# The head of a fused attention and feed-forward kernel: k's squares on other engines, fp32 warm matmuls, another order of the last loads

## Chip, core and metric

One core of a Trainium2 chip runs the whole kernel. The metric is device time in microseconds. Three timed executions of the kernel before took 556.75, 556.82 and 558.07 us, median 556.82.

The engines and their names in the profile: TensorE (PE; its weight loads are PEld), VectorE (DVE), ScalarE (ACT), GpSimd (POOL) and SyncE (SP). POOL issues nearly all loads, SP the transposing DMAs and nearly all stores.

## What is computed

Four batches of 5824 rows and 256 channels. A 256 x 256 attention over channels is made from q and k, applied to v, and the result passes a feed-forward stage without a nonlinearity except one product.

```
qn = q / (norm(q, axis=1) + 1e-6)          # norms run over the 5824 rows
kn = k / (norm(k, axis=1) + 1e-6)
s  = kn^T @ qn / tau                       # 256 x 256 for each batch
a  = exp(s - max); a = a / (sum(a) + 1e-9)
x  = reshape(v @ a)                        # 23296 x 256
out = ((x @ w1) * (x @ w2)) @ w3 @ w_out
```

Inputs and output are fp32; the loads cast to bf16. tau is 1.

## The kernel before

The attention matrix is folded into the weights: for each batch `Wf` = e w1, e w2, scaled by the reciprocals of the sums, so that the main stage needs v alone; w3 and w_out are multiplied once into `W_sb`.

**Main stage.** For each batch there are 12 chunks of up to 512 rows and 8 column blocks `j`: 96 slots. A slot (`emit_ab`, L627) makes `a` and `b` = Wf-block x vT, 128 x 512 each, in two matmuls each; ScalarE casts `a` (L633), VectorE multiplies it with `b` (L644) to `abh`. The banks for `a` and `b` are four, in turn. The product of `abh` with `W_sb` follows some slots later, either plainly (L675, L706) or with seven products in place of eight (L540).

**Order.** The order on every engine is the order of the program, written by a planner: `make_agenda` files pieces of work under a planned time or, for the scores of the next batch, under a slot. The scores of batch 1 are 92 units (23 pairs of row slots, four units each; two of four hold matmuls, L200). `SLOTS0` is the first and last slot of the range over which batch 0 spreads them, and `EARLY` of them are placed before slot `EARLY_SLOT`. Loads for later batches stand in POOL's queue behind `gate` (waits for the newest `abh`) or `hold` (waits for the transpose of a piece of v).

**Head.** Batch 0 has nothing to hide its scores behind. Each of q and k comes in six pieces; pieces 0 to 4 hold 8 slots of 128 rows, piece 5 holds 5 (`LAST` = 5) and a half slot of 64 rows. A DMA waits until the DMA eight places before it in POOL's queue has landed. TensorE runs, as the pieces come:

- `squares`: t^T t of each slot in two 128 x 128 blocks, summed into `S["k"]` and `S["q"]`, whose diagonals are the squared norms (L236);
- `products`: q^T k into G (L248);
- `busy`: matmuls of zeros that only keep TensorE at work (L224).

When k is through, `k_first` multiplies `S["k"]` by the identity (L259), and `k_row` sums it over the partitions by a matmul with ones (L311) and takes four activations to 1/(norm + eps), the row `kr` (L319). `q_first` gets q's squared norms from the diagonal (L328), `q_norm` their reciprocal norms (L339 to L342), `scale` multiplies G by `kr` (L350), `exps` makes `e` (L355). `sum_mm` sums e (L375, its reciprocal L383), `quarter_mm` makes the first folds, 256 columns of w1 and of w2 at a time, which ScalarE (c1 = 0, L431) and VectorE (c1 = 1, L433) scale into `Wf`. Then slot 0 starts. The first two pieces of v are transposed by TensorE in halves (L143), evicted by VectorE (L147) or ScalarE (L145); piece 2 and later by DMA (L166).

The end of the head before, in the program:

```
squares("k", 4, whole)
for sl in (lo, hi):
    squares("q", 4, sl)
    products(4, sl)
squares("k", 5, range(LAST + 1), end=True)
soft0[0]()
parts = [[LAST, 0], [1, 2], [3], [4]]
```

**Tail.** The last half slots of batches 2 and 3 are stored from one tile by two DMAs on SP (L721), the last full row slot from ScalarE's queue (L725).

Of the kernel before, what the change touches and what calls it, by code (L numbers as in the profile page):

```python
# [9 lines left out]
AF = mybir.ActivationFunctionType  # L10
ALU = mybir.AluOpType
F32 = DT.float32
# [13 lines left out]
def kernel(  # L26
# [193 lines left out]
    def busy(k):  # L220

        m = psum.tile([P, 512], F32, name=f"warm_{nc.get_next_instruction_name()}", **bank("ab"))
        for _ in range(k):
            nc.tensor.matmul(m, lhsT=warm[:, :P], rhs=warm, start=True, stop=True, skip_group_check=True)  # L224

    S = {}

    def squares(nm, pi, slots, end=False):

        if nm not in S:  # L230
            S[nm] = psum.tile([P, CT, P], F32, name=f"sq{nm}_0", **bank("out"))
        t = pieces[nm, 0, pi]
        for i in slots:
            for ct in range(CT):
                cs = slice(ct * P, (ct + 1) * P)
                nc.tensor.matmul(  # L236
                    S[nm][:, ct, :], lhsT=t[:, i, cs], rhs=t[:, i, cs],
                    start=(pi == 0 and i == 0 and ct == 0),
                    stop=(end and i == slots[-1] and ct == CT - 1), skip_group_check=True,
                )  # L240

# [12 lines left out]
    def soft_units(n):  # L254
        st = {}

        def k_first():
            d = work.tile([P, CT, P], F32, tag="sq", name="dk", bufs=2)
            nc.vector.tensor_mul(d, S["k"], ident.unsqueeze(1).to_broadcast([P, CT, P]))  # L259
            st["ksq"] = d.rearrange("p c t -> p (c t)")  # L260

        def scaled_first():
            scale(0)
            q_norm(st["ss"])
            scale(1)
            exps(0)
            exps(1)

# [143 lines left out]
            for c2 in range(CT):  # L412
                fold_mm((w, c1, h * 512, (h + 1) * 512), c2, tag, i % 2 == 0 or (n == 0 and i == 7))

        def quarter_mm(lo, c1, c2):

            if c2 == 0:
                tag = "ab" if lo == 0 else "out"
                st[lo, c1] = psum.tile([P, 2, 256], F32, name=f"quarter_{lo}_{c1}", **bank(tag))
            m = st[lo, c1]  # L420
            for w in range(2):
                nc.tensor.matmul(
                    m[:, w, :], lhsT=st["e"][:, c2, c1 * P : (c1 + 1) * P], rhs=w12[:, c2, w, lo : lo + 256],
                    start=(c2 == 0 and w == 0), stop=(c2 == CT - 1 and w == 1), skip_group_check=True,
                )
            if c2 == CT - 1:
                for o in (0, P) if lo == 0 else (slice(0, 256),):
                    cols = slice(o, o + P) if lo == 0 else o
                    dst, src = Wf[n][:, c1, :, lo : lo + 256][:, :, cols], m[:, :, cols]
                    if c1 == 0:  # L430
                        nc.scalar.activation(out=dst, in_=src, func=AF.Copy, scale=st["rs"][:, c1 : c1 + 1])  # L431
                    else:
                        nc.vector.tensor_scalar_mul(dst, src, st["rs"][:, c1 : c1 + 1])  # L433

        def first_folds():
            sum_mm(0)
            for c1 in range(CT):
                quarter_mm(0, c1, 0)
            sum_mm(1)
            for c1 in range(CT):  # L440
                quarter_mm(0, c1, 1)

        def second_quarter():
            for c1 in range(CT):
                for c2 in range(CT):
                    quarter_mm(256, c1, c2)

        if n == 0:
            return [k_first, k_row, q_first, scaled_first, first_folds, second_quarter, sum_start] + [lambda i=i: fold(i) for i in range(4, 8)]

        return (
            [(0.0, 0.0, norms), (0.1, 2.4, totals)]
# [23 lines left out]
        agenda.append((t, seq[0], cost, fn))  # L476

    out_tiles = {}
    lefts = {}
    pend = []  # L480

# [205 lines left out]
    def emit_out(b, c, j, ab, only=None):  # L687

        small = c == NCH - 1
        if small:  # L690
            lhs = [ab[:, :P]]
            if b % 2 == 1:
                lhs.append(lefts[b // 2][:, j, :, :].rearrange("p b t -> p (b t)")[:, P : P + 2 * LEFT])
        else:
            lhs = [ab[:, i * P : (i + 1) * P] for i in range(4)]
        if j == 0:
            out_tiles[b, c] = [
                psum.tile([P, 2, D], F32, tag=tag, name=f"o_{b}_{c}_{tag}", bufs=1)
                for tag in ((("out0", "out2") if b == B - 1 else ("out0", "out1"))[: len(lhs)] if small else ("out0", "out1"))
            ]  # L700
        tl = out_tiles[b, c]
        for s, lhsT in reversed(list(enumerate(lhs))) if small and b == B - 1 else enumerate(lhs):
            if only is not None and s != only:
                continue
            h, o = (s, 0) if small else divmod(s, 2)
            nc.tensor.matmul(  # L706
                tl[h][:, o, :], lhsT=lhsT, rhs=W_sb[:, j, :],
                start=(j == 0 and o == 0), stop=(j == FT - 1 and (small or o == 1)),
                skip_group_check=True,
            )  # L710
        clock[0] += len(lhs) * (D * MM_COL + MM_FIX)
        if j == FT - 1:
            o = work.tile([P, 4, D], F32, tag="o_sb", name=f"osb_{b}_{c}", bufs=3)
            rows = out[b * N : b * N + NT * P, :].rearrange("(p i) c -> p i c", i=NT)
            if small:
                if b % 2 == 1 and only != 0:
                    o2 = work.tile([P, D], F32, tag="kr", name=f"oleft_{b}", bufs=1)
                    nc.vector.tensor_copy(o2, tl[1][:, 0, :])
                    for m in (b - 1, b):
                        k = (m - b + 1) * LEFT  # L720
                        nc.sync.dma_start(out=out[m * N + NT * P : (m + 1) * N, :], in_=o2[k : k + LEFT, :])  # L721
                if only != 1:
                    nc.scalar.copy(o[:, 0, :], tl[0][:, 0, :])
                    other = nc.scalar if b == B - 1 else nc.sync
                    other.dma_start(out=rows[:, NT - 1, :], in_=o[:, 0, :])  # L725
            else:
                nc.scalar.copy(o[:, 0:2, :], tl[0])
                nc.vector.tensor_copy(o[:, 2:4, :], tl[1])
                nc.sync.dma_start(out=rows[:, 4 * c : 4 * c + 4, :], in_=o)
            if only is None:  # L730
                del out_tiles[b, c]
# [4 lines left out]


    half = PIECE // 2
    busy(10)
    raw = {}  # L740
    for nm in "kq":
        new_piece(nm, 0, 0)
# [39 lines left out]
        load_piece("k", 0, pi)  # L782
        load_piece("q", 0, pi)
    load_piece("k", 0, 4)
    load_piece("q", 0, 4, (half,))
    load_piece("k", 0, 5)
    soft0 = soft_units(0)
    whole = range(PIECE)
    lo, hi = range(half), range(half, PIECE)
    for sl in (lo, hi):  # L790
        squares("k", 0, sl)
        busy(2)
    for sl in (lo, hi):
        squares("q", 0, sl)
        products(0, sl)
    for pi in range(1, 4):
        squares("k", pi, whole)
        if pi < 3:
            busy(2)
        squares("q", pi, whole)  # L800
        products(pi, whole)
    load_piece("q", 0, 5, (1, 3, 4))
    new_piece("v", 0, 0)
    load_part("v", 0, 0, 0, half)
# [5 lines left out]
    load_piece("v", 0, 2)  # L810
    nc.gpsimd.dma_start(out=wout_sb, in_=moe_w_out.rearrange("(lh ll) c -> ll lh c", ll=P))
    nc.gpsimd.dma_start(out=w3_bf, in_=w3r)
    squares("k", 4, whole)
    for sl in (lo, hi):
        squares("q", 4, sl)
        products(4, sl)
    squares("k", 5, range(LAST + 1), end=True)
    soft0[0]()
    parts = [[LAST, 0], [1, 2], [3], [4]]
    for i, sl in enumerate(parts):  # L820
        end = i == len(parts) - 1
        squares("q", 5, sl, end=end)
        if end:
            soft0[2]()
        products(5, sl, end=end)
        if i == 0:
            soft0[1]()
    soft0[3]()
    soft0[6]()
    busy(3)  # L830
    transpose_half_on_pe(0, 0, 0, False)
    soft0[4]()

# [9 lines left out]
        else:  # L843
            nc.vector.tensor_copy(W_sb[:, jt, :], m[:, :D])

    SLOTS0, SLOTS = (36, 78), (4, 71)
    EARLY, EARLY_SLOT = 32, 46
    COMB, W_SLOT = 39, 32
    by_slot = []

# [15 lines left out]
    def make_agenda(b):  # L866
# [3 lines left out]
        if b == 0:  # L870
            at(0.5, 0.87, soft0[5])
            for i in range(4):
                at((1.7, 2.6, 3.5, 3.9)[i], 0.43, soft0[7 + i])
            at(4.6, 0.5, lambda: transpose_half_on_pe(0, 0, 1, False))
            at(7.0, 0.5, lambda: transpose_half_on_pe(0, 1, 0, True))
            at(8.0, 0.5, lambda: transpose_half_on_pe(0, 1, 1, False))
            at(15.0, 0.0, transpose_w3)
            at(15.0, 0.0, lambda: transpose_piece(0, 2))
# [9 lines left out]
            moves = [m for m in moves if m[1] < B]  # L888

        for nm, m, pi, t in moves:  # L890
            if (nm, m, pi) in (("qk", 1, 0), ("qk", 1, 2)):
                at(t, 0.0, lambda i=2 + pi // 2: hold(vTs[0][0][:1, i * PIECE, 0, :1]))
            at(t, 0.0, gate)
            if nm == "qk":
                at(t, 0.0, lambda m=m, pi=pi: load_qk(m, pi))
            else:
                at(t, 0.0, lambda m=m, pi=pi: load_piece("v", m, pi))
                at(t + 4.0, 0.0, lambda m=m, pi=pi: transpose_piece(m, pi))
# [81 lines left out]
```

## Time and profile before

| | |
|---|---|
| profiled execution | 557.51 us |
| its span, first to last instruction | 555.5 us |
| median of three timed executions | 556.82 us |
| PE busy | 543.3 us (98% of the span) |
| DVE, ACT, POOL busy | 421.1, 366.7, 305.4 us |
| mean granted TensorE clock | 0.998 |
| first matmul of slot 0 | 37.54 us |
| first load issued by POOL | 1.23 us |

Busy is the time in which an engine had an instruction at work; it says nothing on whether that work was needed or waited for. TensorE's matmuls overlap in the records: a matmul of 128 columns lasts 219 ns, yet 16 in a row start and end within 1.06 us. So the start-to-start distance is the price of one, and the duration shows when its result is there.

A timeline line reads: start, duration, engine, line of the program, operation, written tile <- read tiles, shape, how many merged; in brackets the idle time of the engine before it, and what ended that.

The windows of the head show what each engine does there (busy us of each window):

| window, us | PE | DVE | ACT | POOL | GB/s |
|---|---|---|---|---|---|
| 0 to 10 | 7.48 | 3.27 | 2.33 | 5.66 | 212 |
| 10 to 20 | 7.80 | 0.00 | 0.00 | 2.15 | 213 |
| 20 to 30 | 8.95 | 0.00 | 0.00 | 3.39 | 208 |
| 30 to 40 | 8.64 | 4.81 | 5.13 | 6.93 | 171 |
| 40 to 50 | 9.92 | 6.89 | 7.36 | 0.00 | 208 |
| 50 to 60 | 10.00 | 7.96 | 6.66 | 0.00 | 167 |

### The profile page before, as it was taken

The page shows a single profiled execution, that of the slowest core. Times are in us where ns is not written, and L with a number is a line of the kernel's source. Part 1 is how long each engine was busy: PE and PEld are TensorE (multiplying, and loading weights), DVE is VectorE, ACT ScalarE, POOL GpSimd, SP SyncE. Part 2 cuts the span into 40 slices and gives each one's busy share as a digit, 9 for nine tenths or more (in the row PEclk, how much of TensorE's full clock was granted, in tenths as well). Part 3 has the DMA queues.
Part 4 walks back from the last instruction along what each step waited for, and adds up shares of the span by engine and source line. Part 5 has one row for each costly group of instructions (what it writes and reads, how often), then busy time and mean ns, then how long its engine had stood idle before and what let it go on. Part 6 is the DMA issues. An engine that isn't in the chain of part 4 may idle for free.

```text
span 555.5 us, 12406 instructions
## 1 busy us (share of the span) xinstructions
PE 543.3 (98%) x4697; PEld 355.7 (64%) x4697; DVE 421.1 (76%) x766; ACT 366.7 (66%) x740; POOL 305.4 (55%) x258
## 2 busy tenths in 40 slices
PE   7899999999999999999999999999999999999997
PEld 5764577666666666666667566666666666666665
DVE  2047748799976797888876688888877688888984
ACT  1046647688866877877766778787766566666663
POOL 4260020867789588898887588898977400010000
PEclk9999999999999999999999999999999999999999
DMA  9999988987566977675555767875651245343102
GB/s 212 211 182 209 159 153 199 219 181 136 127 147 153 181 148 163 134 159 131 121 127 133 153 133 167 174 142 118 153 114 39 81 110 125 87 112 84 77 39 95
DMA packets 75115, 77.60 MB, mean 140 GB/s; under 512 B 54192, under 2 KB 58800, under 8 KB 75056
## 3 DMA queue, kind: packets, MB, share of 16 engines
q0 software_dynamic: 15760, 38.93, 40.4%
q1 hardware_dynamic: 59008, 37.23, 24.0%
q8 instruction: 36, 0.59, 0.4%
q10 hardware_dynamic: 288, 0.66, 0.4%
q14 instruction: 23, 0.19, 0.1%
HBM read 78.91 MB, written 23.86 MB: 185 GB/s over the span
## 4 chain that ended last, share of the span: by engine, by line
PE 86%; DMA 9%; POOL 1%; ACT 1%; DVE 1%; issue 1%; POOLq 0%; ACTq 0%
PE a L627 27%; PE b L627 27%; PE prodA L540 12%; PE prodC L540 6%; PE G L200 5%; DMA k<-in_k_dram 4%; PE prodB L540 3%; DMA v<-in_v_dram 2%; PE fold L398 2%; DMA q<-in_q_dram 2%; PE o_out L706 2%; PE w L837 1%; DMA vT<-v 1%; POOL k L120 1%; POOL q L120 0%
## 5 line engine op out<-in xcount | busy, mean ns | idle before, releaser
L644 DVE TENSOR_TENSOR abh<-as,b 128x512 bf16<-128x512 bf16 x352 | 239.9, 684 | 85.1 <-ACT as L633 81.5
L633 ACT CAST as<-a 128x512 bf16<-128x512 f32 (+1 forms) x384 | 215.8, 563 | 93.3 <-PE a L627 63.4
L627 PE MATMUL a<-vT,Wf 128*128 128x512 bf16 x704 | 209.4, 379 | 0.4 <-ACT Wf L431 0.4
L627 PE MATMUL b<-vT,Wf 128*128 128x512 bf16 x704 | 209.4, 379 | 0.0
L627 PEld LDWEIGHTS <-Wf 128*128 128x128 bf16 x1536 | 141.4, 98 | 101.5 <-issue 0.8
L540 PEld LDWEIGHTS <-S 128*128 128x128 bf16 x1248 | 82.6, 98 | 34.3
L212 DVE TENSOR_TENSOR acc<-acc,sq 128x512 f32<-128x512 f32 x132 | 91.5, 693 | 2.7 <-ACT sq L197 1.9
L550 ACT COPY osb<-prodA 128x256 f32<-128x256 f32 x156 | 58.1, 373 | 42.7 <-PE prodA L540 42.2
L559 POOL TENSOR_TENSOR S<-abh,abh 128x1024 bf16<-128x1024 bf16 x29 | 61.8, 2131 | 31.5 <-DVE abh L644 16.4
L540 PEld LDWEIGHTS <-abh 128*128 128x128 bf16 x936 | 62.0, 98 | 25.7 <-issue 0.2
L562 POOL TENSOR_TENSOR S<-S,abh 128x1024 bf16<-128x1024 bf16 x29 | 61.7, 2128 | 1.9
L562 POOL TENSOR_TENSOR S<-abh 128x1024 bf16<-128x1024 bf16 x29 | 61.8, 2132 | 0.1
L562 POOL TENSOR_TENSOR S<-abh,S 128x1024 bf16<-128x1024 bf16 x29 | 61.8, 2133 | 0.1
L615 POOL COPY gate_t<-abh 1x1 bf16<-1x1 bf16 x39 | 7.3, 186 | 79.9 <-DVE abh L644 79.7
L200 PE MATMUL G<-k,q 128*128 128x256 bf16 x276 | 48.3, 273 | 0.9 <-DMA k<-in_k_dram 0.9
L540 PE MATMUL prodA<-comb_T,S 128*128 128x128 bf16 x624 | 47.6, 219 | 0.0
L197 ACT ACTIVATE sq<-q 128x512 f32<-128x512 bf16 x69 | 43.8, 634 | 0.0
L197 ACT ACTIVATE sq<-k 128x512 f32<-128x512 bf16 x69 | 43.5, 631 | 0.0
L553 DVE TENSOR_TENSOR osb<-prodC,osb 128x256 f32<-128x256 f32 x78 | 32.5, 417 | 0.0
L619 POOL COPY gate_t<-vT 1x1 bf16<-1x1 bf16 x2 | 0.4, 178 | 55.0 <-DVE abh L644 37.6
L200 PEld LDWEIGHTS <-q 128*128 128x128 bf16 x276 | 23.6, 98 | 4.2 <-issue 1.0
L540 PE MATMUL prodB<-W_sb,abh 128*128 128x128 bf16 x312 | 23.8, 219 | 0.1
(128 smaller groups left out, 449.6 us busy)
## 6 DMA issues: line engine op xcount, KB each, us to landing
out_dram<-osb SPq DMA_DIRECT2D x44, 512.0 KB, 3.4
k<-in_k_dram POOLq DMA_DIRECT2D x19, 512.0 KB, 8.7
v<-in_v_dram POOLq DMA_DIRECT2D x19, 512.0 KB, 5.7
q<-in_q_dram POOLq DMA_DIRECT2D x18, 512.0 KB, 5.8
w_wout<-in_moe_w_dram POOLq DMA_DIRECT2D x1, 2048.0 KB, 22.8
k<-in_k_dram POOLq DMA_DIRECT2D x4, 320.0 KB, 7.1
v<-in_v_dram POOLq DMA_DIRECT2D x4, 320.0 KB, 4.8
q<-in_q_dram POOLq DMA_DIRECT2D x3, 320.0 KB, 5.3
```

Source lines behind the costliest of these rows:

```text
L197: nc.scalar.activation(out=sqs[0][:, :, part, :], in_=src[:, o : o + 2, :], func=AF.Square)
L200: nc.tensor.matmul(G[:, ct, :], lhsT=qt[:, i, ct * P : (ct + 1) * P], rhs=kt[:, i, :], start=(pr == 0 and part == 0 and ct == 0), stop=(pr ...
L212: nc.vector.tensor_add(accs[n], accs[n], sqs[0][:, part - 2])
L398: nc.tensor.matmul(m, lhsT=st["e"][:, c2, c1 * P : (c1 + 1) * P], rhs=w12[:, c2, w, lo:hi], start=(c2 == 0), stop=(c2 == CT - 1),)
L540: nc.tensor.matmul(st[nm][:, i, :], lhsT=a[:, j, i * P : (i + 1) * P], rhs=w[j], start=(first and j == 0 and i == 0), stop=(j == 3), skip_ ...
L550: nc.scalar.copy(quarter(r, d), st["A"])
L553: nc.vector.tensor_add(quarter(r, d), st[nm], quarter(r, d))
L559: adder.tensor_add(x, a21, a22)
L562: adder.tensor_sub(x, u, w)
L627: nc.tensor.matmul(t[:, :n], lhsT=Wf[b][:, ct, w, j * P : (j + 1) * P], rhs=rhs_of(b, c, ct), start=(ct == 0), stop=(ct == CT - 1),)
L633: nc.scalar.copy(a_sb[:, :n], tiles[0][:, :n])
L644: nc.vector.tensor_mul(ab, a_sb, tiles[1])
```

## The change

1. The squares of k's slots 0 to 35 (pieces 0 to 3, and half of piece 4) leave TensorE. ScalarE squares two slots at a time, VectorE adds them into one PSUM tile `kacc`. `k_early` joins its two halves, and `k_first` adds them to the diagonal that the remaining ten slots give; the sum over partitions by `k_row` is as before.
2. The zero matmuls in bf16 are replaced by fp32 matmuls of ones with 512 columns (`busy_long`), 3 at the start, then 2, 1 and 2 behind the pieces 0, 1 and 2. The ones behind the first exponentials' inputs stay bf16, 2 instead of 3.
3. k's piece 5 is loaded ahead of the second half of q's piece 4, which comes in two parts; `k_row` stands ahead of q's piece 5.
4. Both scalings of G stand ahead of q's norm.
5. The first folds take 128 columns, evicted at once; the next 128 follow before slot 0.
6. Batch 1's scores start at slot 37 with 28 units before slot 46.
7. One TensorE transpose of v is evicted by VectorE instead of ScalarE.
8. The store of the last batch's half slot goes to ScalarE's queue behind its row store.

The two uses of `hold` stay, only written otherwise. The diff, cut:

```diff
+    def busy_long(k):
+        m = psum.tile([P, 4, P], F32, name=f"warm_{nc.get_next_instruction_name()}", **bank("ab"))
+        for _ in range(k):
+            nc.tensor.matmul(
+                m, lhsT=ones_pp, rhs=ones_pp.unsqueeze(1).to_broadcast([P, 4, P]), start=True, stop=True,
+                skip_group_check=True,
+            )
+    def add_k_squares(pi, slots):
+        for i in slots[::2]:
+            src = pieces["k", 0, pi][:, i : i + 2, :]
+            if not kacc:
+                kacc.append(psum.tile([P, 2, C], F32, name="kacc", tag="out0", bufs=1))
+                nc.scalar.activation(out=kacc[0], in_=src, func=AF.Square)
+                continue
+            sq = work.tile([P, 2, C], F32, tag="sq", name=f"ksq_{pi}_{i}", bufs=2)
+            nc.scalar.activation(out=sq, in_=src, func=AF.Square)
+            nc.vector.tensor_add(kacc[0], kacc[0], sq)
...
+        def k_early():
+            st["kk"] = work.tile([P, C], F32, tag="kk", name="kk", bufs=1)
+            nc.vector.tensor_copy(st["kk"], kacc[0][:, 0, :])
+            nc.vector.tensor_add(st["kk"], kacc[0][:, 1, :], st["kk"])
...
             nc.vector.tensor_mul(d, S["k"], ident.unsqueeze(1).to_broadcast([P, CT, P]))
-            st["ksq"] = d.rearrange("p c t -> p (c t)")
+            d = st["ksq"] = d.rearrange("p c t -> p (c t)")
+            nc.vector.tensor_add(d, d, st["kk"])
         def scaled_first():
-            scale(0)
+            for ct in range(CT):
+                scale(ct)
             q_norm(st["ss"])
-            scale(1)
...
         def first_folds():
-            sum_mm(0)
+            for c2 in range(CT):
+                sum_mm(c2)
+                for c1 in range(CT):
+                    narrow_fold(0, P, c1, c2)
             for c1 in range(CT):
-                quarter_mm(0, c1, 0)
-            sum_mm(1)
-            for c1 in range(CT):
-                quarter_mm(0, c1, 1)
+                for c2 in range(CT):
+                    narrow_fold(P, 2 * P, c1, c2)
...
-                        nc.sync.dma_start(out=out[m * N + NT * P : (m + 1) * N, :], in_=o2[k : k + LEFT, :])
+                        store = lambda m=m, k=k, queue=nc.sync: queue.dma_start(
+                            out=out[m * N + NT * P : (m + 1) * N, :], in_=o2[k : k + LEFT, :]
+                        )
+                        if m < B - 1:
+                            store()
+                        else:
+                            last_rows.append(store)
...
+                    if last_rows:
+                        last_rows.pop()(queue=nc.scalar)
...
-    busy(10)
+    busy_long(3)
...
-    load_piece("q", 0, 4, (half,))
+    new_piece("q", 0, 4)
+    load_part("q", 0, 4, 0, half)
     load_piece("k", 0, 5)
+    load_part("q", 0, 4, half, half + 2)
+    load_part("q", 0, 4, half + 2, PIECE)
...
-    for sl in (lo, hi):
-        squares("k", 0, sl)
-        busy(2)
+    add_k_squares(0, whole)
     for sl in (lo, hi):
         squares("q", 0, sl)
         products(0, sl)
+    busy_long(2)
     for pi in range(1, 4):
-        squares("k", pi, whole)
-        if pi < 3:
-            busy(2)
+        add_k_squares(pi, whole)
         squares("q", pi, whole)
         products(pi, whole)
+        if pi < 3:
+            busy_long(pi)
...
-    squares("k", 4, whole)
-    for sl in (lo, hi):
+    add_k_squares(4, lo)
+    soft0[7]()
+    squares("k", 4, hi)
+    squares("q", 4, lo)
+    products(4, lo)
+    squares("k", 5, range(LAST + 1), end=True)
+    soft0[0]()
+    for sl in (range(half, half + 2), range(half + 2, PIECE)):
         squares("q", 4, sl)
         products(4, sl)
-    squares("k", 5, range(LAST + 1), end=True)
-    soft0[0]()
-    parts = [[LAST, 0], [1, 2], [3], [4]]
...
+    soft0[1]()
+    for sl in ([LAST, 0], [1, 2], [3]):
+        squares("q", 5, sl)
+        products(5, sl)
+    squares("q", 5, [4], end=True)
+    soft0[2]()
+    products(5, [4], end=True)
     soft0[3]()
     soft0[6]()
-    busy(3)
+    busy(2)
...
-    SLOTS0, SLOTS = (36, 78), (4, 71)
-    EARLY, EARLY_SLOT = 32, 46
+    SLOTS0, SLOTS = (37, 78), (4, 71)
+    EARLY, EARLY_SLOT = 28, 46
...
-            at(7.0, 0.5, lambda: transpose_half_on_pe(0, 1, 0, True))
+            at(7.0, 0.5, lambda: transpose_half_on_pe(0, 1, 0, False))
```

More of the change, by code (lines that the diff above doesn't have):

```diff
@@ L224, in busy @@
             nc.tensor.matmul(m, lhsT=warm[:, :P], rhs=warm, start=True, stop=True, skip_group_check=True)
+    def busy_long(k):
[5 more added lines that the diff above has]
+            )
+    kacc = []
+    def add_k_squares(pi, slots):
[8 more added lines that the diff above has]
+            nc.vector.tensor_add(kacc[0], kacc[0], sq)
     S = {}
@@ L237, in squares @@
                     S[nm][:, ct, :], lhsT=t[:, i, cs], rhs=t[:, i, cs],
-                    start=(pi == 0 and i == 0 and ct == 0),
+                    start=((pi, i) == ((4, half) if nm == "k" else (0, 0)) and ct == 0),
                     stop=(end and i == slots[-1] and ct == CT - 1), skip_group_check=True,
@@ L413, in fold, with narrow_fold @@
                 fold_mm((w, c1, h * 512, (h + 1) * 512), c2, tag, i % 2 == 0 or (n == 0 and i == 7))
-        def quarter_mm(lo, c1, c2):
+        def narrow_fold(lo, hi, c1, c2):
             if c2 == 0:
-                tag = "ab" if lo == 0 else "out"
-                st[lo, c1] = psum.tile([P, 2, 256], F32, name=f"quarter_{lo}_{c1}", **bank(tag))
+                tag = "ab" if lo < 256 else "out"
+                st[lo, c1] = psum.tile([P, 2, hi - lo], F32, name=f"narrow_{lo}_{c1}", **bank(tag))
             m = st[lo, c1]
@@ L422, in quarter_mm @@
                 nc.tensor.matmul(
-                    m[:, w, :], lhsT=st["e"][:, c2, c1 * P : (c1 + 1) * P], rhs=w12[:, c2, w, lo : lo + 256],
+                    m[:, w, :], lhsT=st["e"][:, c2, c1 * P : (c1 + 1) * P], rhs=w12[:, c2, w, lo:hi],
                     start=(c2 == 0 and w == 0), stop=(c2 == CT - 1 and w == 1), skip_group_check=True,
@@ L426, in quarter_mm @@
             if c2 == CT - 1:
[L427 to L433, printed above, removed]
+                dst = Wf[n][:, c1, :, lo:hi]
+                if c1 == 0:
+                    nc.scalar.activation(out=dst, in_=m, func=AF.Copy, scale=st["rs"][:, c1 : c1 + 1])
+                else:
+                    nc.vector.tensor_scalar_mul(dst, m, st["rs"][:, c1 : c1 + 1])
         def first_folds():
-            sum_mm(0)
+            for c2 in range(CT):
+                sum_mm(c2)
+                for c1 in range(CT):
+                    narrow_fold(0, P, c1, c2)
             for c1 in range(CT):
-                quarter_mm(0, c1, 0)
-            sum_mm(1)
-            for c1 in range(CT):
-                quarter_mm(0, c1, 1)
+                for c2 in range(CT):
+                    narrow_fold(P, 2 * P, c1, c2)
         def second_quarter():
@@ L445, in second_quarter @@
                 for c2 in range(CT):
-                    quarter_mm(256, c1, c2)
+                    narrow_fold(256, 512, c1, c2)
         if n == 0:
-            return [k_first, k_row, q_first, scaled_first, first_folds, second_quarter, sum_start] + [lambda i=i: fold(i) for i in range(4, 8)]
+            return [k_first, k_row, q_first, scaled_first, first_folds, second_quarter, sum_start, k_early] + [lambda i=i: fold(i) for i in range(4, 8)]
         return (
@@ L478 @@
     out_tiles = {}
+    last_rows = []
     lefts = {}
@@ L720, in emit_out @@
                         k = (m - b + 1) * LEFT
-                        nc.sync.dma_start(out=out[m * N + NT * P : (m + 1) * N, :], in_=o2[k : k + LEFT, :])
+                        store = lambda m=m, k=k, queue=nc.sync: queue.dma_start(
[3 more added lines that the diff above has]
+                            store()
+                        else:
+                            last_rows.append(store)
                 if only != 1:
@@ L812 @@
     nc.gpsimd.dma_start(out=w3_bf, in_=w3r)
-    squares("k", 4, whole)
-    for sl in (lo, hi):
+    add_k_squares(4, lo)
[6 more added lines that the diff above has]
+    for sl in (range(half, half + 2), range(half + 2, PIECE)):
         squares("q", 4, sl)
         products(4, sl)
-    squares("k", 5, range(LAST + 1), end=True)
-    soft0[0]()
-    parts = [[LAST, 0], [1, 2], [3], [4]]
[L820 to L827, printed above, removed]
+    soft0[1]()
[5 more added lines that the diff above has]
+    products(5, [4], end=True)
     soft0[3]()
     soft0[6]()
-    busy(3)
+    busy(2)
     transpose_half_on_pe(0, 0, 0, False)
@@ L872, in make_agenda @@
             for i in range(4):
-                at((1.7, 2.6, 3.5, 3.9)[i], 0.43, soft0[7 + i])
+                at((1.7, 2.6, 3.5, 3.9)[i], 0.43, soft0[8 + i])
             at(4.6, 0.5, lambda: transpose_half_on_pe(0, 0, 1, False))
-            at(7.0, 0.5, lambda: transpose_half_on_pe(0, 1, 0, True))
+            at(7.0, 0.5, lambda: transpose_half_on_pe(0, 1, 0, False))
             at(8.0, 0.5, lambda: transpose_half_on_pe(0, 1, 1, False))
@@ L890, in make_agenda @@
         for nm, m, pi, t in moves:
-            if (nm, m, pi) in (("qk", 1, 0), ("qk", 1, 2)):
-                at(t, 0.0, lambda i=2 + pi // 2: hold(vTs[0][0][:1, i * PIECE, 0, :1]))
+            if nm == "qk" and m == 1 and pi in (0, 2):
+                at(t, 0.0, lambda pi=pi: hold(vTs[0][0][:1, (2 + pi // 2) * PIECE, 0, :1]))
             at(t, 0.0, gate)
```

## The prediction

> **What bounds the kernel now.** I read the busy table first (PE 98% of the span), then who TensorE waits for, the chain of waits of the first 75 us, and the instructions around each place where that chain leaves TensorE. After the first `a` matmul at 37.54 us TensorE loses almost nothing; the waits from there on are two (engine, what it waits for: us in total, times, longest):
>
> ```profile
> PE G L200 <- DMA k<-in_k_dram: 0.9, 1, 0.9
> PE a L627 <- ACT Wf L431: 0.4, 1, 0.4
> ```
>
> So the time is: when the first `a` starts, plus about 514 us of packed TensorE work, plus the tail. The chain of the head (start us, us, what):
>
> ```profile
> 4.51 16.54 DMA k<-in_k_dram
> 21.34 10.29 DMA q<-in_q_dram
> 31.96 0.44 PE G L248 x4
> 32.40 0.45 PE row L311 x2
> 33.73 0.52 ACT kr L319
> 35.45 0.52 ACT e L355
> ...
> 37.01 0.48 ACT Wf L431
> 37.54 0.61 PE a L627 x2
> ```
>
> Until 31.6 the loads set the pace; the DMA engines move 208 to 213 GB/s through the first 30 us, so nothing before that is worth anything unless it finishes loads earlier. From 31.6 on it is a dependent chain: last q, k's row of sums, four activations, the exponentials, first folds, first `a`. The timeline of the hand-over:
>
> ```profile
> 31.67 0.28 PE L236 MATMUL sqq<-q 128*128 128x128 bf16 x2 [0.42 <-DMA q<-in_q_dram]
> ...
> 33.66 0.28 PE L236 MATMUL sqq<-q 128*128 128x128 bf16 x2
> ...
> 33.97 0.29 DVE L328 CUSTOM_DVE_ANT_0 dq<-sqq,ident 128x128 f32<-128x128 f32 x1 [2.37 <-PE sqq L236]
> ...
> 35.45 0.91 ACT L355 ACTIVATE e<-s,r 128x256 bf16<-128x256 f32 x2 [0.44 <-DVE r L342]
> ...
> 36.57 0.60 PE L422 MATMUL quarter<-w,e 128*128 128x256 bf16 x4
> ```
>
> The last part of q was issued at 27.51 and took 5.0 us to land, so it is there at 32.5; its squares start at 33.66. For 2.0 us from 31.67 TensorE is without a gap and behind the loads.
>
> Two more places outside the head:
>
> ```profile
> 49.23 0.59 PE L627 MATMUL b<-vT,Wf 128*128 128x512 bf16 x2
> 105.33 0.60 PE L200 MATMUL G<-k,q 128*128 128x256 bf16 x4 [0.85 <-DMA k<-in_k_dram]
> 551.70 1.12 SPq L721 DMA_DIRECT2D out_dram<-oleft  x2
> 551.86 0.36 ACTq L725 DMA_DIRECT2D out_dram<-osb  x1
> ```
>
> **Part by part.**
>
> *Squares of k off TensorE.* 36 slots x 2 = 72 matmuls; 16 of them take 0.90 us (10.98 to 11.88), so 4.0 us leave TensorE. All lie before 27 us, where TensorE waits for q anyway (3.7 us in four waits): worth 0. In their place come 18 squares on ScalarE (631 ns each, the row of the later k squares, 11.4 us) and 17 adds on VectorE (693 ns, 11.8 us). Cover: VectorE sits idle 22.9 us before 31.18, ScalarE 26.2 before 32.87. The last two slot pairs hang on k piece 4, landed at 25.95 (issued 7.25, 18.7 to land): squares to 27.6, adds to 28.3, the two joining operations to about 29.1 (0.4 each, as the 128x256 multiply). k's diagonal cannot start before k piece 5, so this is hidden; were it not, each 0.7 us late would first eat the slack of the row below.
>
> *Order of loads and of the row.* Now k piece 5 comes before the second half of q piece 4. It should land near 29.0 (before: 30.28), q piece 4's two new parts at 29.7 and 30.2, the same bytes by then. TensorE: k5 squares to 29.6, first part (0.22 + 0.44) to 30.3, second to 31.0, the row (0.45) to 31.4, and q piece 5 waits for its load as before (31.64). What falls out of the gapless 2.0 us after 31.67 is the row: the final squares move from 33.66 to 33.21. POOL's queue: one more DMA, and the ninth and later issues each stand until the one eight earlier has landed. Counting on with those landings, the last weights before v go out about 0.2 us later (w3 at 36.7 instead of 36.5), since the weight issues run back to back at 0.7 us either way.
>
> *The price of the split.* The DMA records of the trace give 173 ns for a 2 KB packet, 98 for 1 KB, 60 for 512 B. Half a piece of q was 128 packets of 2 KB: 128 x 173 / 16 engines = 1.38 us; as two parts it is 256 x 98 / 16 = 1.57. By the row the q loads end 0.19 later. The Trainium skill speaks both ways: "DMA: Bandwidth & Descriptors" (Specifications) lets anything from 512 B up run at line rate, which makes it 0 and the gain 0.45; "Perfetto Trace Analysis" (DMA Optimizations) warns of overhead under 2 KB without a price, and even at the 512 B row (240 ns per 2 KB) it would be 0.5, which takes the gain away. I take the row: final squares at 33.40, 0.26 earlier.
>
> *From the last squares to e.* Now k's row is ready by 33.5, so both scalings follow the diagonal at once and the norm of q comes behind them on VectorE: diagonal from +0.31 to +0.82, scalings 0.34 apart, then add and reciprocal at the old spacing; e starts 1.93 after the squares (before 35.45 - 33.66 = 1.79). So 35.33 against 35.45: 0.12 earlier.
>
> *Narrow first folds.* The second half of the row sums waited for four 256-column matmuls (36.08 to 36.52) though e was ready at 36.36. Four of 128 columns take 0.22, so it now waits for e: 36.30 instead of 36.52. The fold in front of ScalarE's eviction shrinks too, and the reciprocal (0.21 behind the sums, 0.17 long) becomes the releaser: eviction at about 36.75 instead of 37.01. It still covers 256 elements a row (0.42). The 8 matmuls of columns 128 to 256 (0.45) fit beside it. First `a` at **37.28: 0.26 earlier**. The first weights must be there at 35.95; I put the second one's landing at 35.4.
>
> *Warm matmuls in fp32.* Eight of 512 columns; the fp32 row has 256 columns in 0.45, so 0.9 each. Except for the first three, they stand where TensorE waits for q and all end before its landing (11.4 against 13.15, 16.7 against 18.8, 23.2 against 23.5): 0. But the longest pauses grow from 1.65 us (17.16 to 18.81) to about 2.1. Before, 128 columns take 0.055 us after every pause; at the start the first warm matmuls came every 0.43 us instead of 0.216 until 4.19. The Trainium skill ("TensorE: Matmul & The Clock Gate", HAM oscillation) asks for no pause over about 3.4 us, which clears this; its next section tells of clocks that fell on short pauses, which does not. No row here has a 2.1 us pause. Between 0 and one cold stretch like the start's (2.9 us at half rate, 1.5 us lost); I take 0, near the 1.65 us row.
>
> *A transpose's eviction from ScalarE to VectorE.* Before, ScalarE's 1.01 us copy delayed its next cast, VectorE then stood 1.10 us, came late with the following product, and `b` at 49.23 started 0.20 after TensorE was free. On VectorE the copy fits that idle stretch: **-0.20**.
>
> *Scores of batch 1 paced.* 28 units instead of 32 before slot 46 move the first pair of k piece 2 from slot 46 to slot 48, about 4 us of packed work later. That load landed at 105.28 and hangs on a chain of DMAs (hold, v piece 3, its transpose, hold), which the head does not shift. TensorE gets there at 108, so the whole wait goes: **-0.85**. Next late would be k piece 3 (111.6 against slot 56, after 121): no. Starting at slot 37 protects the first pair, whose k landed at 83.4, 0.05 before use.
>
> *Tail.* The last store on SP starts at 552.24 and lands at 554.55, the row store on ScalarE's queue at 554.35. Behind the latter the moved store can start at 552.22 and ends issuing 0.24 sooner. Between -0.25 and +0.15; I take **-0.1**.
>
> **Sum**: -0.26 - 0.20 - 0.85 - 0.10 = -1.4. Against the profiled execution (557.51; span 555.5 and 2.0 around it) 556.1; that execution was 0.7 above the median, so **555.4**.
>
> **Rivals.** About 0.3% (1.67 us) is what a measurement can tell from no change.
> - *Head gain held up* (0.20): v pieces bound it. Slot 32 at 75.63 needs a transpose landed at 74.94, v piece 1 lands some 0.5 before its transpose; with loads 0.2 later little of 0.46 may pass. -0.95: 555.9.
> - *Loads end no later* (0.22): packets overlap, the split costs nothing: head -0.5 to -0.6, and stores gain their 0.25. -1.9: 554.9, faster.
> - *Clock falls at the hand-over* (0.13): between 33.7 and 37.3 TensorE has about 1.6 us of pauses (before some 1.45, with one warm matmul more), the `a` stage starts at half rate. One stretch is +1.5, a second +3.0; slower than before once over 1.4, beyond 0.3% once over 3.1. Two stretches: 558.4. For it: the thinner filling; against: nothing cold after 4.2 us before.
> - *As summed* (0.45): own range 554.9 to 556.0.
>
> Range 554.2 to 557.6. Faster by over 0.3% needs under 555.15: most of the second rival and a third of the sum's own spread, 0.33; slower 0.12; within 0.55.
>
> **What would show it.** First `a` at 37.1 to 37.4; final q squares at 33.2 to 33.4; no wait on k at L200's successor near 105; the 0.2 gap near 49 gone; 55 ns a matmul after every pause. It is wrong if q piece 5 lands after 32.2, if `a` waits for vT at slot 32, or if the first `a` and `b` run at 0.43 a matmul.

## The result, and the profile after

The changed kernel took 556.14 us (median of 15 runs, 555.53 to 556.96) against 557.38 of the kernel before beside it (15 runs, 556.58 to 558.07). The ratio is 0.9978 with a 95% interval of 0.9970 to 0.9986, or -1.24 us with an interval of -0.8 to -1.7: a small gain. The interval excludes no change, but the 0.22% lies below the 0.3% that I had put as what a measurement can tell. In the profiled executions it is 555.64 us (span 553.9) against 557.51 (span 555.5).

Who TensorE waits for in the first 38 us of the kernel after (us in total, times, longest); from 37.7 us to the end the same view names nobody, where it named k for 0.9 and ScalarE's first copy of `Wf` for 0.4 before:

```profile
PE sqq L259 <- DMA q<-in_q_dram: 4.0, 4, 1.3
...
PE sum L404 <- ACT e L384: 0.6, 1, 0.6
```

The chain of the head after (start us, us, what):

```profile
13.31 15.71 DMA k<-in_k_dram
...
30.67 5.22 DMA w<-in_moe_w_dram
...
35.93 0.33 PE narrow L451 x3
...
36.59 0.48 ACT Wf L458
...
37.12 0.61 PE a L656 x2
```

Before, the chain ran through q, k's row and `e`. Now the last thing that comes late is a weight: the second of the first weights, issued at 30.67, releases the folds at 35.89, though `e` started at 34.98. The timeline of the hand-over:

```profile
29.07 0.84 PE L259 MATMUL sqk<-k 128*128 128x128 bf16 x12 [0.24 <-DMA k<-in_k_dram]
...
33.15 0.28 PE L259 MATMUL sqq<-q 128*128 128x128 bf16 x2
...
34.98 0.91 ACT L384 ACTIVATE e<-s,r 128x256 bf16<-128x256 f32 x2 [0.54 <-DVE r L371]
...
35.61 0.65 PE L451 MATMUL narrow<-w,e 128*128 128x128 bf16 x4
```

The merged row at 35.61 hides the wait: four matmuls of 128 columns, which take 0.38 us where nothing holds them, show 0.65, and no bracket. Only the chain says why. And the three places outside the head:

```profile
48.20 0.59 PE L656 MATMUL a<-vT,Wf 128*128 128x512 bf16 x2
48.64 0.60 PE L656 MATMUL b<-vT,Wf 128*128 128x512 bf16 x2
...
107.19 0.60 PE L200 MATMUL G<-k,q 128*128 128x256 bf16 x4
550.69 0.67 ACTq L750 DMA_DIRECT2D out_dram<-oleft  x1
```

`a` and `b` near 48 are 0.43 apart, the packed distance: the gap of 0.20 is gone. The scores that waited at 105.33 now stand at 107.19, and their k landed at 103.51: no bracket. In the tail the moved store takes 0.67 us to issue.

Every span can be cut at the first `a` and at ScalarE's last copy of output. That separates the head, the packed stage and the tail, and is the measure for the experiments (us, one profile each):

| kernel | last q squares | `e` | first `a` | first `a` to last copy | last copy to end |
|---|---|---|---|---|---|
| before | 33.66 | 35.45 | 37.54 | 513.92 | 4.01 |
| before, again (e4_base) | 33.66 | 35.46 | 37.55 | 514.90 | 3.98 |
| pacing alone (e1_pace) | 33.64 | 35.47 | 37.55 | 512.93 | 4.01 |
| pacing alone (e10_pace) | 33.18 | 34.98 | 37.06 | 512.93 | 3.99 |
| pacing, eviction (e2_outside) | 33.38 | 35.18 | 37.26 | 512.87 | 3.99 |
| after | 33.15 | 34.98 | 37.12 | 512.76 | 4.00 |
| after, again (e5_after) | 33.38 | 35.21 | 37.77 | 512.74 | 3.99 |
| after, again (e11_after) | 33.19 | 35.02 | 37.51 | 512.73 | 4.00 |
| head and tail alone (e3_head) | 33.38 | 35.22 | 37.71 | 514.75 | 4.42 |

The two halves of the change stand apart in it. The packed stage becomes 1.2 us shorter in all three profiles of the changed kernel, and 1.0 with the old head. The head gets no shorter: first `a` is at 37.06 to 37.55 with the old head (five profiles, mean 37.39) and at 37.12 to 37.77 with the new one (four, mean 37.53). The 0.42 us that the two first profiles show between them is the spread of one execution to the next.

### The profile page after: what moved, and what is told of

It reads as the page before. It is cut to its first block, busy times and chain, and to the rows that moved or that the text cites. A ratio compares the mean times of both kernels' runs of the same rounds, so it can differ in the third digit from the quotient of the medians.

```text
span 553.9 us, 12324 instructions
## 1 busy us (share of the span) xinstructions
PE 542.9 (98%) x4623; PEld 353.3 (64%) x4630; DVE 435.3 (79%) x787; ACT 377.0 (68%) x757; POOL 305.5 (55%) x259
## 4 chain that ended last, share of the span: by engine, by line
PE 92%; DMA 6%; POOL 1%; DVE 0%; ACT 0%; issue 0%; POOLq 0%
PE a L656 28%; PE b L656 28%; PE prodA L569 12%; PE prodC L569 6%; PE G L200 5%; PE prodB L569 3%; DMA k<-in_k_dram 3%; PE o L704 3%; PE fold L427 2%; DMA q<-in_q_dram 2%; PE o_out L735 2%; PE w L878 1%; DMA w<-in_moe_w_dram 1%; PE narrow L451 0%; DVE abh L673 0%
## 5 line engine op out<-in xcount | busy, mean ns | idle before, releaser
L200 PE MATMUL G<-k,q 128*128 128x256 bf16 x276 | 47.0, 273 | 0.0
```

Source lines behind the costliest of these rows:

```text
L200: nc.tensor.matmul(G[:, ct, :], lhsT=qt[:, i, ct * P : (ct + 1) * P], rhs=kt[:, i, :], start=(pr == 0 and part == 0 and ct == 0), stop=(pr ...
```

## The experiments

Each ratio is to the kernel before, timed on the same chip, with its 95% interval.

**The parts outside the head, one by one.** The pacing alone, on the kernel before:

```diff
-    SLOTS0, SLOTS = (36, 78), (4, 71)
-    EARLY, EARLY_SLOT = 32, 46
+    SLOTS0, SLOTS = (37, 78), (4, 71)
+    EARLY, EARLY_SLOT = 28, 46
```

> The kernel before with only the pacing of batch 1's scores (slots from 37, 28 units before slot 46). Theory (the parts add, and the load of k piece 2 is bound by DMAs alone): first `a` at 37.5 as before, no wait of TensorE on k near 105 us, and 0.85 to 1.0 us less: ratio 0.9982 to 0.9985. Rival (the wait is an accident of the one profile, or comes back at k piece 3): ratio 0.9995 to 1.0, or a new wait between 105 and 125 us.

Measured: 556.06 us, 0.9971 (0.9960 to 0.9983). The stage shrank from 513.92 to 512.93. From 37.7 us on, TensorE waits only once in e1_pace, 0.4 us for ScalarE's first copy of `Wf`. Two constants are thus enough for all of the gain that the whole change brings. The gap near 49 is still there (48.61 to 49.24 is 0.63 where 0.43 is packed):

```profile
48.61 0.59 PE L627 MATMUL a<-vT,Wf 128*128 128x512 bf16 x2
49.24 0.59 PE L627 MATMUL b<-vT,Wf 128*128 128x512 bf16 x2
```

With the eviction on VectorE as well:

```diff
-            at(7.0, 0.5, lambda: transpose_half_on_pe(0, 1, 0, True))
+            at(7.0, 0.5, lambda: transpose_half_on_pe(0, 1, 0, False))
```

> The pacing, and the transpose's eviction on VectorE; the head as before. Theory: the gap of 0.2 us before `b` near 49 is gone, slot 9 starts 0.2 earlier than before, 1.05 to 1.2 us less in all: ratio 0.9979 to 0.9982. Rival (an eviction on VectorE only moves the stall): a gap of 0.15 us or more elsewhere between 43 and 51, ratio as with the pacing alone.

Measured: 556.22 us, 0.9977 (0.9968 to 0.9986). The timeline of e2_outside at the same place is packed:

```profile
48.33 0.59 PE L627 MATMUL a<-vT,Wf 128*128 128x512 bf16 x2
48.76 0.59 PE L627 MATMUL b<-vT,Wf 128*128 128x512 bf16 x2
```

But here 0.13 of it comes back 5 us later, where `a` at 53.51 is followed by `b` at 54.07, 0.56 apart. With the old head the stage gains 0.06 by this edit. With the new head, where no such gap follows, the stage is 0.19 shorter than with the pacing alone (512.93 to 512.74), but these two differ in the head as well, and no run has the new head without this edit alone. The timed runs cannot resolve either number.

The head alone, with the tail: the changed kernel with both edits above undone.

> The changed head and tail alone; pacing and eviction as before. Theory (head saves 0.4, but k piece 2 hangs on DMAs): first `a` at 37.1, and the wait on k near 105 grows from 0.85 to about 1.3, so next to nothing is left at the end: ratio 0.9995 to 1.0. Rival (the head also brings the DMA chain forward): wait stays at 0.9, ratio 0.9992 or less.

Measured: 557.31 us, 0.9997 (0.9987 to 1.0007): nothing. First `a` came at 37.71, not at the expected 37.1. TensorE's waits from 37.7 us on:

```profile
PE a L656 <- DMA vT<-v: 1.1, 1, 1.1
PE G L200 <- DMA k<-in_k_dram: 0.4, 1, 0.4
```

The first is slot 32, which waited for the transpose of v until 77.05. That is the place which the rival "head gain held up" named, though this head had gained nothing that could be held up. Its last weight load went out at 37.64 (before: 36.51), but in e5_after, further on, it goes out at 37.71 and slot 32 does not wait; so this is one execution's late transpose as far as the runs show. The wait on k is 0.4 and not the expected 1.3, since TensorE came there after the loss of 1.1. The kernel before, once more:

> The kernel before once more, unchanged: how far a second profile and the ratio move by themselves. Theory: ratio 0.9995 to 1.0005, wait on k near 105 between 0.5 and 1.2. Rival (the profiled wait is a property of one execution): wait under 0.3.

Measured: 557.98 us, 1.0006 (0.9997 to 1.0014). Its waits from 37.7 us on:

```profile
PE G L200 <- DMA k<-in_k_dram: 0.9, 1, 0.9
PE tr_I-619_620 L143 <- DMA v<-in_v_dram: 0.8, 1, 0.8
```

The wait on k is the kernel's own, 0.9 in both executions. The one on v is not: a single profile of the same program can be longer by 0.8 us because one load came late, and this is two thirds of the 1.24 that was to be explained.

**Why the head gains nothing.** The changed kernel again, unedited:

> The changed kernel once more. Theory (the first folds now wait for the second first weight, whose landing varies): first `a` between 37.1 and 37.7, the narrow folds waiting for w in the later case, and the ratio 0.997 to 0.9985, no better than with the pacing alone. Rival (head gains 0.4 in every run): first `a` at 37.0 to 37.2, ratio 0.997 or less.

Measured: 556.51 us, 0.9986 (0.9977 to 0.9995), first `a` at 37.77. The chain of e5_after:

```profile
30.89 5.65 DMA w<-in_moe_w_dram
...
36.59 0.33 PE narrow L451 x3
...
37.77 0.60 PE a L656 x2
```

`e` started at 35.21, 0.24 earlier than in the kernel before, and the first folds waited 0.53 us for the second weight. In all four profiles of the new head the chain runs through it: it releases the folds at 35.89, 36.54, 36.28 (e11_after) and 36.47 (e3_head). So I tried to bring the weights forward: the first pair ahead of v's first half, and q's norm between the two scalings, as before.

```diff
-    load_part("v", 0, 0, 0, half)
     for f0, f1 in ((0, 256), (256, 512), (512, F)):
         nc.gpsimd.dma_start(out=w12[:, :, 0, f0:f1], in_=w1r[:, :, f0:f1])
         nc.gpsimd.dma_start(out=w12[:, :, 1, f0:f1], in_=w2r[:, :, f0:f1])
+        if f0 == 0:
+            load_part("v", 0, 0, 0, half)
...
-            for ct in range(CT):
-                scale(ct)
+            scale(0)
             q_norm(st["ss"])
+            scale(1)
```

> The changed kernel with the two first weights issued ahead of v's first half, and q's norm between the two scalings again. Theory (weights and VectorE's order bound e and the folds): no wait on w, e 0.1 us sooner after the last squares of q (1.73 instead of 1.83), first `a` at 36.9 to 37.1; at the end 0 to 0.3 us less than the changed kernel, as later loads may hold it up. Rival (v's transpose now comes late and takes it back): TensorE waits for v before the sums, first `a` at 37.3 or later.

Measured: 558.58 us, 1.0017 (1.0006 to 1.0028), slower than the kernel before. `e` came at 34.92, but now v's first half was late: issued at 30.72 instead of 29.30, it took 7.3 us instead of 4.2, and its transpose stands ahead of the folds on TensorE. The timeline of e6_weights:

```profile
38.06 0.99 PE L143 MATMUL tr_I-475_476<-ident_b,v 128*128 128x128 bf16 x8 [3.75 <-DMA v<-in_v_dram]
...
40.66 1.05 PE L656 MATMUL a<-vT,Wf 128*128 128x512 bf16 x2
```

The pause also cost the clock. The windows of e6_weights (stretch in us, its length, then busy us and instructions of PE, PEld, DVE, ACT, POOL, the granted TensorE clock, DMA share, GB/s):

```profile
38.00:39.00 1.00, 0.94 (x11) 0.94 (x12) 0.00 (x0) 0.00 (x0) 0.70 (x1) 0.57 1.20 197
39.00:40.00 1.00, 1.00 (x15) 1.00 (x13) 0.77 (x2) 0.05 (x1) 1.00 (x2) 0.50 1.22 209
...
41.00:42.00 1.00, 1.00 (x5) 0.40 (x4) 0.39 (x1) 0.26 (x1) 0.00 (x0) 0.72 1.08 214
```

The clock is at 1.00 before 38 and from 42 on; between them (0.57, 0.50, 0.50 and 0.72 in four windows of 1 us) TensorE loses 1.7 us of work at full clock, what half the clock for 3.4 us would cost, and the first pair of `a` takes 1.05 us instead of 0.61. This is what the third rival would look like; the changed kernel, with a clock of 1.00 in each 4 us window from 8 to 40 us of its three profiles, shows none of it.

**Single parts of the head, taken back.** All squares of k on TensorE again, in the changed kernel:

```diff
-    add_k_squares(0, whole)
+    for sl in (lo, hi):
+        squares("k", 0, sl)
...
-        add_k_squares(pi, whole)
+        squares("k", pi, whole)
...
-    add_k_squares(4, lo)
-    soft0[7]()
-    squares("k", 4, hi)
+    squares("k", 4, whole)
```

> The changed kernel with all squares of k on TensorE again (order of loads, row, warm matmuls and folds as changed). Theory (TensorE waits for loads until 29 us): last squares of q 4.0 to 4.3 us after k piece 5 lands, as in the changed kernel, time within 0.2 us of it. Rival (the squares were a backlog): last squares 0.5 us or more later.

Measured: 556.39 us, 0.9983 (0.9974 to 0.9992), first `a` at 37.12 as in the changed kernel's first profile. Moving 72 matmuls off TensorE is worth nothing in time, as priced. The chain of e7_k_on_pe:

```profile
35.13 0.52 ACT e L383
...
35.89 0.24 PE narrow L450 x4
...
37.12 0.60 PE a L655 x2
```

Here the weight was in time, and one can read what the new order costs without it: 1.99 us from `e` to `a`.

Without the fp32 matmuls between the pieces (they compute nothing of the output; the three at the start stay):

```diff
-    busy_long(2)
     for pi in range(1, 4):
...
-        if pi < 3:
-            busy_long(pi)
```

> The changed kernel without the fp32 warm matmuls behind pieces 0, 1 and 2, so TensorE pauses 2.3 to 3.1 us three times. Theory (these pauses are too short for the clock to fall): 128 columns in 0.055 us after every pause, first `a` and time as the changed kernel within 0.2 us. Rival (the clock falls): 0.107 us for 128 columns behind some pause, first `a` later by 0.3 to 1.5 us.

Measured: 556.02 us, 0.9975 (0.9965 to 0.9985). The timeline of e8_no_warm:

```profile
13.15 1.07 PE L259 MATMUL sqq<-q 128*128 128x128 bf16 x16 [3.37 <-DMA q<-in_q_dram]
...
18.13 1.74 PE L259 MATMUL sqq<-q 128*128 128x128 bf16 x16 [2.16 <-DMA q<-in_q_dram]
...
24.02 1.07 PE L259 MATMUL sqq<-q 128*128 128x128 bf16 x16 [1.43 <-DMA q<-in_q_dram]
```

Sixteen squares took 1.07 us after a pause of 3.37 and 1.74 after a later one of 2.16: the clock did fall. The windows of e8_no_warm, in the same columns:

```profile
18.00:19.00 1.00, 0.87 (x10) 0.88 (x11) 0.90 (x2) 0.48 (x1) 0.53 (x1) 0.66 1.07 217
19.00:20.00 1.00, 1.00 (x11) 0.94 (x9) 0.42 (x1) 0.00 (x0) 0.00 (x0) 0.50 1.07 213
```

The changed kernel's clock is 1.00 there, so the fp32 matmuls do keep the clock. But the slow stretch ends before the next load lands, and first `a` is at 37.05: what they keep is worth nothing here.

The second half of q's piece 4 in one load instead of two:

```diff
-    load_part("q", 0, 4, half, half + 2)
-    load_part("q", 0, 4, half + 2, PIECE)
+    load_part("q", 0, 4, half, PIECE)
...
-    for sl in (range(half, half + 2), range(half + 2, PIECE)):
+    for sl in (hi,):
```

> The changed kernel with q piece 4's second half in one load again (no split; one DMA less in POOL's queue). Theory (the split costs no landing time, but the extra DMA sends everything behind it out later): last squares of q no later than 4.3 us after k piece 5 lands, the second first weight issued 0.2 us or more earlier than in the changed kernel, no wait on w, first `a` 37.0 to 37.2. Rival (the split is what lets TensorE work earlier): last squares 0.3 us or more later, first `a` at 37.4 or later.

Measured: 556.33 us, 0.9985 (0.9977 to 0.9994). The timeline of e9_whole_q:

```profile
30.65 0.62 PE L259 MATMUL sqq<-q 128*128 128x128 bf16 x8 [0.47 <-DMA q<-in_q_dram]
...
34.06 0.28 PE L259 MATMUL sqq<-q 128*128 128x128 bf16 x2
```

From k's last squares (29.33) to q's last it is 4.73 us, with the split 4.08 (29.07 to 33.15). So the split earns 0.65 there, and `e` starts at 35.86 without it. The folds then found their weights and `a` followed at 37.86, about where e5_after was: what the split earns, the wait for the weight can take again. The expectation was missed: I had thought that one DMA less would bring the second weight's issue forward, but it went out at 30.89 (30.67 with the split).

**Repeats, and wide folds.** The pacing alone and the changed kernel, once more each, beside the changed kernel with its first folds 256 columns wide:

> The pacing alone once more, beside the changed kernel on the same chip. Theory (all of the gain is the pacing): time within 0.3 us of the changed kernel, no wait on k near 105. Rival (the head adds its 0.4): 0.4 us or more above the changed kernel.

> The changed kernel beside the pacing alone. Theory: first `a` at 37.1 if the second first weight is there in time, at 37.7 if not; ratio to before 0.997 to 0.9985. Rival as for the pacing alone.

> The changed kernel with the first folds of 256 columns again. Theory: first `a` 0.2 us later after e than in the changed kernel (2.3 instead of 2.1 us from the start of e), where no weight is waited for; time 0 to 0.2 us more. Rival (the folds are hidden beside the reciprocal and the evictions): the distance from e to the first `a` stays at 2.1.

Measured: 556.34 us, 0.9983 (0.9972 to 0.9993) for the pacing alone; 556.18, 0.9986 (0.9977 to 0.9994) for the changed kernel; 556.69, 0.9995 (0.9983 to 1.0007) with wide folds. In the last the weight came at 36.80, the folds waited 0.93 us, and first `a` was at 38.19. So the distance from `e` cannot be read there; from the weight's landing to first `a` it is 1.39, against 1.23 in the four profiles with narrow folds that waited. The first shows the old head in a good execution. The chain of e10_pace:

```profile
34.98 0.52 ACT e L355
...
37.06 0.61 PE a L627 x2
```

The same `e` and an earlier `a` than the changed kernel's best. In that execution the first slot of q's piece 5 was not late, and TensorE ran from k's last squares (30.30) to q's (33.18) without the gap of 0.42 that the kernel before shows at 31.67.

Only e3_head and e6_weights have intervals that do not overlap with the changed kernel's 0.9970 to 0.9986, and both are the slower ones. None is told from it as faster, the pacing alone included.

## Why the prediction came out as it did

The sum, -1.4 us, stands against -1.24 measured. The forecast 555.4 lies 0.7 below the 556.14, since the kernel before was 557.38 in that comparison and 556.82 in the runs that it started from. That the sum came so near is in part luck: -0.36 of it (head and tail) did not come, and the pacing brought 0.14 more than its price. The first profile's `a` at 37.12, inside the forecast 37.1 to 37.4, was luck too: the next two were at 37.77 and 37.51. Term by term:

- **Pacing, -0.85: right, and a little small.** The stage became 0.99 shorter by it, and the scores that waited now come 2.7 to 3.7 us after their k (107.19 against 103.51 in the changed kernel, 107.80 against 105.10 in e1_pace). The bracket in front of the matmul at 105.33 gave 0.85, but a stall costs more than its idle time: the eight matmuls at 103.44 should have taken 8 x 0.109 = 0.87, so the next was due at 104.31 and came 1.02 later. The last record's tail of some 0.17, which lies beside the next matmul when all is packed, is not in the idle time.
- **Eviction, -0.20: right for the gap, open for its worth.** The gap is gone; with the old head most of it reappeared as one of 0.13 near 54 us and 0.06 was left, and with the new head the 0.19 is not separated from the head.
- **Tail, -0.1: wrong, 0.** From the last copy to the end it is 3.99 to 4.00 us in the three profiles of the changed kernel and 3.98 to 4.01 with the store unmoved (4.42 in e3_head alone). I had the moved store end issuing 0.24 sooner; it starts about where I put it (0.81 after the last copy's start, forecast 0.76), but its issue takes 0.67 us (0.36 for the row store on that queue), so it ends 0.12 later (1.48 against 1.36 after that start).
- **Head, -0.26: wrong, nothing.** The step that failed is "the first weights must be there at 35.95; I put the second one's landing at 35.4". It released the folds at 35.89 to 36.54, and they wanted it from 35.7 (after) or 35.9 (e5_after) on. What went before held: final squares at 33.15 to 33.38 (predicted 33.40; the old head 33.18 to 33.66), means 33.28 against 33.50, though the ranges overlap; 1.83 from there to `e` (predicted 1.93), means 35.11 against 35.31. The narrow folds are worth 0.09 where the weight is in time: `e` to `a` takes 1.99 in e7_k_on_pe and 2.08 with the old folds in e10_pace. With the weight late it takes 2.14, 2.56 and 2.49 in the three profiles of the changed kernel. So some 0.3 us was won ahead of `a`, and as much or more was lost to a load whose slack I had at half a microsecond. That landing was estimated from one execution, and of the old head, where it came at 35.13. The late weight held POOL's queue too: the next load waited for its landing and went out 0.3 after it, so w3 went out at 37.06 to 37.71 instead of the predicted 36.7.
- **Squares of k at 0: right** (e7_k_on_pe). What this move may have done to the weights stands below. **fp32 matmuls at 0: right** in time. The longest wait for q became 1.3 us, not 2.1, since the fp32 matmuls fill more of it, and the granted clock stayed up. But my reason for taking 0 was weak: e8_no_warm went cold after a pause of 2.16 us. The Trainium skill's rule that I set against it ("TensorE: Matmul & The Clock Gate", HAM oscillation), no pause over about 3.4 us, does not cover this case; what the page's next section, on PSUM-queue cycling, tells of clocks that fall on short pauses is nearer to the run, though its pauses have another cause.
- **Price of the split: wrong.** By the packet records q was to end 0.19 later. Its last part landed at 32.20, 4.1 us after its issue at 28.09, and in e9_whole_q, with one load, at 32.46 (27.87 and 4.6). No price is to be seen; the Trainium skill's rule that I set aside ("DMA: Bandwidth & Descriptors", Specifications), full rate from 512 B, was nearer. It made no gain of 0.45 either, because the last q no longer binds: from k's piece 5, landed at 29.02, TensorE is packed for 4.08 us, so k's landing and the work behind it set the final squares. For the same reason the sign "wrong if q piece 5 lands after 32.2" was a bad one: it landed at 32.20 to 32.39 in the four profiles of the new head, and the final squares came as predicted.

Of the rivals, "head gain held up" was right that the head's gain is lost and had the place wrong: the weights took the gain, not v. "Loads end no later" was right on the loads and wrong on what they release. "Clock falls at the hand-over" did not happen, and e6_weights shows how it would have looked.

Open: why the second weight is late. It is issued at about the same time with both heads (30.53 before, 30.67 after). The landings of all profiles (issue plus time to landing) show that it is not chance alone. The queues of the page of the changed kernel give a candidate, packets that the profile calls "instruction", 36 of 16 KB each in the run:

```profile
q8 instruction: 36, 0.59, 0.4%
```

One of them, of some 0.9 to 1.0 us, falls into the head's last loads:

| profiles | k's squares on TensorE | such a packet starts | second weight lands | folds wait for it |
|---|---|---|---|---|
| old head, five | all | 29.50 to 30.11 | 34.94 to 35.23 | no |
| e7_k_on_pe | all | 29.43 | 35.58 | no |
| new head (after, e5, e11, e3), and e12_wide | last ten slots | 33.63 to 34.49 | 35.89 to 36.80 | yes |
| e9_whole_q | last ten slots | 33.59 | 35.09 | no |
| e8_no_warm | last ten slots | 35.11 | 35.30 | no |

In each of the five profiles that waited, the weight lands 2.26 to 2.31 us after the start of that packet. (In e6_weights, where the weights are issued ahead of v, it starts at 35.47 and v's half lands at 38.02.) And the packet comes 3.5 us or more later in every profile in which k's squares have left TensorE. So a possible reading is that the move of the squares, priced at 0, brought this packet into the landing of the weights. It is not shown: no run moves the packet alone, e9_whole_q has it at the same time and its weight in time, and the variants are one profile each.

## What to carry to other kernels

Where a chain of waits is shortened by some tenths of a microsecond, list every load that the new end needs and how much slack each has, and do not take its landing from the old order: the second weight landed within 0.29 us in five profiles of the old head, and 0.7 to 1.6 us later in the new one. One profile of each kernel cannot tell a head gain of 0.3 us (first `a` moved by 0.49 between profiles of the old head): cut the span at fixed points and profile the unchanged kernel again first. A stall that returns in each execution at the same place, as k's near 105, is worth more than shaving a chain, and here two constants removed it.

## What was not expected of the hardware

- The clock fell after a pause of 2.16 us but not after one of 3.37 us five microseconds earlier (e8_no_warm). So the length of a single pause did not decide here. Between the two lay only some 2.8 us of work; whether that is the reason no run tests.
- In e6_weights a pause of 3.75 us was followed by a loss of clock worth 3.4 us at half rate.
- A load's time to landing can grow by much more than its issue moves: v's first half took 4.2 us in the changed kernel and 7.3 when it was issued 1.4 us later, behind two weight loads (e6_weights, one profile).
- The same program's first `a` came at 37.12, 37.51 and 37.77 in three profiles, each 1.23 us after the landing of the second weight.
